# Block solve joins on four corners of the array with one joined tile per chunk, w0 loads and x_scr stores per pair of groups

## The chip, the cores and the metric

The kernel runs on one core of one Trainium2 chip. The metric is the device time of one execution in microseconds; for the kernel before the median of three runs is 1325.73 us (1323.58 to 1325.76).

## What is computed

A recurrent attention over 768 steps for 32 heads (4 batches of 8) with a state of 40x40 per head, and behind it two MLP layers of 320 to 2048 to 320 on all 3072 tokens, all in float32. The second layer uses an ELU in place of the squared ReLU.

```python
for t in range(S):
    y[:, :, t] = np.einsum('bhd,bhde->bhe', rt, state)
    Sa = np.einsum('bhde,bhe->bhd', state, at)
    state_decay = state * wt[:, :, None, :] - np.einsum('bhd,bhe->bhde', Sa, bt)
    state = state_decay + np.einsum('bhd,bhe->bhde', vt, kt)
x = attn_out.transpose(0, 2, 1, 3).reshape(B * S, H * D)
h = np.maximum(x @ w_in, 0.0); x = h * h @ w_out
h = x @ w_in2; g = np.where(h > 0, h, np.exp(np.minimum(h, 0)) - 1); out = g @ w_out2
```

## The kernel before

The 768 steps are cut into 12 chunks of 64 (`C`, `NC`), and the 32 heads into four groups `u` of 8 (`U`, `HU`); two groups form a pair `p`, and the members of a pair are told apart by `g = u % 2`. Within a chunk the recurrence becomes a triangular system per head, with a matrix of 64x64. A chunk goes through these stages:

- *prep*: running products of the decay (`scan`), scaled copies of a and r split into three bf16 planes and stored to DRAM, and k and b scaled (`kb_rows`).
- *gram*: for each group the 64x64 products (`gram`); the part for the solve is copied to `bs` and stored to `b_scr` by ACT's queue.
- *solve*: the system is cut into two halves of 32 and these into blocks of 16. `block_load` brings all 128 diagonal blocks (32 heads, four each) into a tile `w`, and fifteen `block_step`s on DVE invert them. `block_store` writes one inverse per half in transposed form to `n_scr` and both to `t_scr`, from where SP loads `n1` (tag nt) and the tiles `tb`, in which the inverse of each 32x32 half is put together. What is missing there is the block off the diagonal of each half: minus the product inverse, coupling, inverse. `block_join` makes it by two runs of small matmuls per chunk. The first run multiplies the coupling (`lz`, tag pb, 16 rows, 32 columns of which the left 16 are cleared by POOL) with `n1`; the second multiplies its result `x` with the inverse that stands in `tb`, and the result is copied into `tb`.
- *dynamic*: with the state at the chunk's start, `dyn_f`, `dyn_u`, `dyn_bu` and `dyn_u` again solve for a pair (by `tb`), `dyn_sp`, `dyn_ut` and `dyn_gh` make the second gram, `dyn_y` the outputs, `dyn_s` and `dyn_st` the new state. `w0` holds the decay products: `dyn_y` multiplies the output into it and stores it to `x_scr`, `dyn_s` reads its last column.
- *mlp1* and *mlp2*: the two layers, 24 passes over 256 tokens in float32r with hi and lo parts. They read `x_scr` and `x2_scr`.

In a run of the join `put` and `base` give the places. In the first run a head's two halves lie at rows and columns 0 and 32 of the array; in the second at 0 and 32 for groups with g = 0 and at 64 and 96 for those with g = 1. Each run has 64 matmuls for 32 heads, in two groups of 32 matmuls (`nc.group()`), and each group is copied out of PSUM by itself: two copies of 64 rows in the first run, four of 16 rows in the second. Both groups write one PSUM tile (`accA` for the first two chunks, then tag `at`).

The order of all instructions is written by a planner within the kernel. `at(...)` gives each step a due time from the tables `OFF`, `SHIFT` and `BIAS`; `flush` then simulates five engines and the DMA rings, takes at each engine the ready step with the smallest score, and fixes the resulting order for each engine. A `nc.group()` is one step that isn't broken up. `T_W2` and `T_CL` are the due times at which buffers of the attention's preparation are given to the second layer's weights. The buffer counts that matter here are `TB` (tiles `tb`, three of [128, 16, 32]) and `W0` (two of [40, 8, 65]). The matrix instructions of all stages stand in the trace under line 528, where the planner issues them.

Of the kernel before, what the change touches and what calls it, by code (L numbers as in the profile page):

```python
# [11 lines left out]
F32 = mybir.dt.float32  # L12
# [10 lines left out]
B, H, S, D = 4, 8, 768, 40  # L23
# [23 lines left out]
RP, TB, KB, KS = 1, 3, 3, 1  # L47
GS, LIMIT, FLOOR = 4, 2.0 ** 80, 2.0 ** -50
WPE = True
T_W2, T_CL = 176.1, 213.4  # L50
OFF = {
# [9 lines left out]
}  # L61
SHIFT = {
    "prep": [-252.4, -24.58, -12.17, -10.47, -1.272, -5.026, -6.748, -9.319, -3.061, -9.193, -7.383, -4.819],
# [1396 lines left out]
```

## Time and profile before

| | us |
|---|---|
| median of three runs | 1325.73 |
| profiled execution, its own time | 1321.71 |
| span of the profiled execution | 1319.9 |
| PE busy with matmuls | 1207.2 |
| ACT busy | 792.5 |
| DVE busy | 769.4 |
| POOL busy | 510.3 |

The span runs from the first to the last instruction; the profiled execution is one of its own and lies 4.0 us under the median. The granted clock of TensorE is 0.949 on average over the span. Times in the rows below count from the start of the span. An fp32 matmul of the program stands in the trace as two records, each with its weight load (PEld).

### The profile page before, as it was taken

Reading aid. Unit: us, or ns where it says so; the run is one execution under the profiler, and the core shown is the slowest. Engines: PE = TensorE matmul, PEld = TensorE weight load, DVE = VectorE, ACT = ScalarE, POOL = GpSimd, SP = SyncE. Lnnn points to the kernel's source line nnn. Section 1 sums busy time; section 2 is a strip of 40 time slices with the busy share of each in tenths; the row PEclk is TensorE's granted clock in tenths of the full one; section 3 lists DMA queues with packets and bytes.
Section 4 is the critical chain, followed back from the end, with each engine's and each line's share of the span. In section 5 each row is a group of like instructions: output and inputs, shape, how many; then the busy total and the mean of one; then the engine's idle time right before and its main releaser. Section 6 shows DMA issues by size and latency. Waiting matters only on the chain. (4 is left out here: it accounts for less than half of the span.)

```text
span 1319.9 us, 41548 instructions
## 1 busy us (share of the span) xinstructions
PE 1207.2 (91%) x17409; PEld 1105.7 (84%) x17409; DVE 769.4 (58%) x1434; ACT 792.5 (60%) x1536; POOL 510.3 (39%) x485
## 2 busy tenths in 40 slices
PE   2648779999998999999999999999999999999996
PEld 1536657889897898889888999999999999999995
DVE  6467866756575668665655645578744444444442
ACT  4556576565674657575655546455666666666663
POOL 2341241153363334364334224367633333333332
PEclk9996768897998799999999999999999999999998
DMA  8787786575777475765565434334200010000000
GB/s 268 189 222 207 179 253 153 126 187 150 185 195 164 104 203 130 196 138 160 129 160 136 103 77 135 123 103 124 65 21 20 22 30 21 21 21 22 16 11 18
DMA packets 239570, 157.99 MB, mean 120 GB/s; under 512 B 164112, under 2 KB 212624, under 8 KB 239376
## 3 DMA queue, kind: packets, MB, share of 16 engines
q1 hardware_dynamic: 213072, 148.18, 42.2%
q10 hardware_dynamic: 26304, 7.08, 2.8%
q8 instruction: 139, 2.28, 0.7%
q14 instruction: 55, 0.45, 0.1%
HBM read 114.52 MB, written 40.69 MB: 118 GB/s over the span
## 5 line engine op out<-in xcount | busy, mean ns | idle before, releaser
L528 PE MATMUL h<-xhi,w 128*128 128x256 f32 x1920 | 512.3, 298 | 2.9 <-DVE r L528 1.6
L528 POOL TENSOR_TENSOR glo<-r,ghi 128x512 fp32r<-128x512 f32 x192 | 254.0, 1324 | 413.9 <-ACT ghi L528 219.6
L528 PEld LDWEIGHTS h<-xhi,w 128*128 128x128 f32 x1920 | 357.8, 191 | 22.8 <-DVE r L528 12.7
L528 PE MATMUL h<-xlo,w 128*128 128x256 f32 x1152 | 324.4, 284 | 1.8 <-POOL xlo L528 1.6
L528 PEld LDWEIGHTS h<-xlo,w 128*128 128x128 f32 x1152 | 220.6, 191 | 2.7 <-POOL xlo L528 2.7
L528 ACT ACTIVATE r<-h 128x512 f32<-128x512 f32 x192 | 114.7, 597 | 139.6 <-PE h L528 117.4
L528 DVE SCALAR_TENSOR_TENSOR r<-e,r 128x512 f32<-128x512 f32 x96 | 81.3, 847 | 182.0 <-ACT r L528 180.9
L528 PE MATMUL accA<-w,ghi 128*128 128x320 f32 x768 | 179.1, 315 | 1.9 <-ACT ghi L528 1.9
L528 PE MATMUL accB<-w,ghi 128*128 128x320 f32 x768 | 178.2, 314 | 0.0
L528 DVE TENSOR_TENSOR r<-h,r 128x512 f32<-128x512 f32 x192 | 132.4, 689 | 74.9 <-ACT ghi L528 53.3
L528 PEld LDWEIGHTS accA<-w,ghi 128*128 128x128 f32 x768 | 124.9, 191 | 3.4 <-ACT ghi L528 2.8
L528 PEld LDWEIGHTS accB<-w,ghi 128*128 128x128 f32 x768 | 125.4, 191 | 0.4
L528 PE MATMUL accA<-w,glo 128*128 128x320 f32 x384 | 124.0, 323 | 1.0 <-POOLq L1392 0.6
L528 PE MATMUL accB<-w,glo 128*128 128x320 f32 x384 | 123.2, 321 | 0.0
L528 ACT CAST ghi<-r 128x512 fp32r<-128x512 f32 x96 | 59.0, 615 | 37.2 <-DVE r L528 20.5
L528 DVE SCALAR_TENSOR_TENSOR tt<-tt 128x1 f32<-128x1 f32 (+4 forms) x165 | 71.4, 433 | 15.9 <-DMA tt<-b_scr 8.5
L528 POOL TENSOR_TENSOR kd<-kbt,ks 128x320 f32<-128x320 f32 x42 | 38.1, 908 | 103.1 <-ACT ks L528 101.7
L528 PEld LDWEIGHTS accA<-w,glo 128*128 128x128 f32 x384 | 73.7, 192 | 2.8 <-POOL glo L528 1.1
L528 ACT ACTIVATE ghi<-r 128x512 fp32r<-128x512 f32 x96 | 60.6, 632 | 24.1 <-PE accB L528 21.0
L528 PEld LDWEIGHTS accB<-w,glo 128*128 128x128 f32 x384 | 73.4, 191 | 1.3
L528 ACT ACTIVATE r<-r 128x512 f32<-128x512 f32 x96 | 60.7, 632 | 2.0
L528 ACT COPY gx<-stk 120x1024 bf16<-120x1024 bf16 x48 | 48.5, 1011 | 22.1 <-PE stk L528 13.0
(157 smaller groups left out, 2159.7 us busy)
## 6 DMA issues: line engine op xcount, KB each, us to landing
gy<-ya_scr SPq DMA_DIRECT2D x144, 120.0 KB
rq<-r_scr SPq DMA_DIRECT2D x72, 240.0 KB
cs<-w SPq DMA_DIRECT2D x32, 512.0 KB
kbt<-kbt SPq DMA_DIRECT2D x12, 640.0 KB
cs<-w SPq DMA_DIRECT2D x16, 384.0 KB
b_scr<-bs ACTq DMA_DIRECT2D x48, 128.0 KB
ya_scr<-pl SPq DMA_DIRECT2D x12, 480.0 KB
r_scr<-pl SPq DMA_DIRECT2D x12, 480.0 KB
```

The source lines that it names most:

```text
L528: i = getattr(getattr(self.nc, name), op)(*a, **k)
```

## The change

The join is laid out anew. `b_scr` is filled in the order of `spot(u)`, so that the groups with g = 0 come first and those with g = 1 second, and `side(g)` names each half of the heads. `lz` and `n1` now take all 128 partitions: for each side and half the 16 rows lie at partitions 0, 32, 64 and 96. In both runs a step `n` issues four matmuls at the four corners (rows and columns 0, 32, 64, 96), for 16 values of `n`, in a single group of 64 matmuls. `lz` is packed without the cleared left half; its stationary is still 32 columns wide and reaches into the next head's columns, whose results aren't read. The second run reads the inverse from the right half of `n1` in place of `tb`, with 16 rows contracted in place of 32. For that `n_scr` has 32 columns, ACT's queue stores two kinds of inverse to it, and it is cleared once at the start; it has two buffers for the twelve chunks. The first run's result goes to a tile `xj` by one copy on ACT; the second's is copied out by two copies each on ACT and DVE. The two `tb` tiles of a chunk become one with two buffers (`TB`). `w0` is loaded for a pair of groups at once, with one buffer, and `x_scr` is stored for the pair after the second group's `dyn_y`. All numbers of the planner's tables are replaced.

```diff
--- before.py
+++ after.py
@@ -44,145 +44,146 @@
-RP, TB, KB, KS = 1, 3, 3, 1
+RP, TB, KB, KS = 1, 2, 3, 1
-T_W2, T_CL = 176.1, 213.4
+T_W2, T_CL = 177.1, 222.8
...
@@ -579,7 +580,7 @@
-    n_scr = [dram.tile([NH, 2, 16, 16], F32, name=f"n_scr{c}") for c in range(NC)]
+    n_scr = [dram.tile([NH, 2, 32, 32], F32, name=f"n_scr{c}") for c in range(2)]
@@ -813,6 +814,12 @@
+        def spot(u):
+            return u % 2 * 2 + u // 2
+
+        def side(g):
+            return slice(g * 2 * HU, (g + 1) * 2 * HU)
+
@@ -974,7 +981,7 @@
-            nc.scalar.dma_start(out=ap(b_scr[c][:], u * HU * HB, [[C, C], [HB, HU], [1, C]]), in_=bs[b])
+            nc.scalar.dma_start(out=ap(b_scr[c][:], spot(u) * HU * HB, [[C, C], [HB, HU], [1, C]]), in_=bs[b])
@@ -982,29 +989,29 @@
-            lz = get("pb", 0, [128, NH, 32])
-            n1 = get("nt", 1024, [64, NH, 16])
+            lz = get("pb", 0, [128, NH * HU + 16])
+            x = get("xj", 272, [128, 2 * HU, 16])
+            n1 = get("nt", 528, [128, 2 * HU, 32])
...
-            ex[c, "lz"], ex[c, "n1"], ex[c, "w"] = lz, n1, w
-            nc.gpsimd.memset(flat(lz)[0:64], 0.0)
+            ex[c, "lz"], ex[c, "xj"], ex[c, "n1"], ex[c, "w"] = lz, x, n1, w
+            nc.gpsimd.memset(lz[:, NH * HU:], 0.0)
...
-            for h in range(2):
-                tb = p1.tile([128, NH // 2, 32], F32, tag="tb", bufs=TB, name="tb")
-                ex[c, h, "tb"] = tb
+            ex[c, "tb"] = p1.tile([128, 2, 2 * HU, 32], F32, tag="tb", bufs=TB, name="tb")
...
-            for h in range(2):
-                o = 32 * h
-                nc.sync.dma_start(out=ex[c, "lz"][o:o + 16, :, 16:32], in_=ap(b_scr[c][:], o * C + o + 16, [[C, 16], [HB, NH], [1, 16]]))
-                for g in range(2):
+            for g in range(2):
+                k = g * 2 * HU * HB
+                for o in (0, 32):
...
-                        out=ex[c, h, "tb"][64 - 64 * g:96 - 64 * g, HU * g:HU * g + HU],
-                        in_=ap(b_scr[c][:], (2 * h + g) * HU * HB + 32, [[C, 32], [HB, HU], [1, 32]]))
+                        out=ex[c, "lz"][64 * g + o:64 * g + o + 16, :NH * HU].rearrange("p (n r) -> p n r", r=16),
+                        in_=ap(b_scr[c][:], k + o * C + o + 16, [[C, 16], [HB, 2 * HU], [1, 16]]))
+                nc.sync.dma_start(
+                    out=ex[c, "tb"][64 - 64 * g:96 - 64 * g, g], in_=ap(b_scr[c][:], k + 32, [[C, 32], [HB, 2 * HU], [1, 32]]))
@@ -1014,54 +1021,38 @@
-            w = ex[c, "w"]
+            w, n = ex[c, "w"], n_scr[c % 2]
...
-            nc.scalar.dma_start(out=n_scr[c].rearrange("n h t r -> (n h) t r"), in_=w[::2, 0])
+            for q, i in ((1, 1), (0, 0)):
+                nc.scalar.dma_start(out=ap(n[:], 16 * q, [[1024, 64], [32, 16], [1, 16]]), in_=w[q::2, i])
...
-            for h in range(2):
-                nc.sync.dma_start(out=ex[c, "n1"][32 * h:32 * h + 16], in_=n_scr[c][:, h].rearrange("n t r -> t n r"))
-            for u in range(U):
-                g = u % 2
-                nc.sync.dma_start(
-                    out=ex[c, u // 2, "tb"][64 * g:64 * g + 64, HU * g:HU * g + HU],
-                    in_=t_scr[c % 2][hs(u)].rearrange("n q r t -> (q r) n t"))
+            for g in range(2):
+                nc.sync.dma_start(out=ex[c, "n1"][64 * g:64 * g + 64], in_=n[side(g)].rearrange("n h t x -> (h t) n x"))
+            for g in range(2):
+                nc.sync.dma_start(out=ex[c, "tb"][64 * g:64 * g + 64, g], in_=t_scr[c % 2][side(g)].rearrange("n q r t -> (q r) n t"))
...
-            lz, n1 = ex[c, "lz"], ex[c, "n1"]
-            x = flat(lz)[:, :NH * 16].rearrange("p (n r) -> p n r", n=NH)
-
-            def run(rows, put, l, r, evict):
+            lz, x, n1, tb = ex[c, "lz"], ex[c, "xj"], ex[c, "n1"], ex[c, "tb"]
+
+            def run(rows, l, r):
...
-                    ps = ps_acc.tile([128, NH, 16], F32, tag="accA", name="join")
+                    ps = ps_acc.tile([128, 2 * HU, 16], F32, tag="accA", name="join")
...
-                    ps = ps_at.tile([128, NH, 16], F32, tag="at", name="join")
-                for k in range(2):
-                    with nc.group():
-                        for n in range(16 * k, 16 * k + 16):
-                            for o in (0, 32):
-                                nc.tensor.matmul(out=ps[put(o, n):put(o, n) + rows, n], lhsT=l(o, n), rhs=r(o, n), start=True, stop=True)
-                    evict(ps, k, slice(16 * k, 16 * k + 16))
-
-            def first(ps, k, n):
-                for g in range(2):
-                    o, m = 64 * g, slice(16 * k + HU * g, 16 * k + HU * g + HU)
-                    (nc.scalar.copy if k else nc.vector.tensor_copy)(out=x[o:o + 64, m], in_=ps[0:64, m])
-
-            def second(ps, k, n):
-                for g in range(2):
-                    o, m, h = 64 * g, slice(16 * k + HU * g, 16 * k + HU * g + HU), slice(HU * g, HU * g + HU)
-                    nc.scalar.copy(out=ex[c, k, "tb"][o:o + 16, h, 16:32], in_=ps[o:o + 16, m])
-                    nc.vector.tensor_copy(out=ex[c, k, "tb"][o + 32:o + 48, h, 16:32], in_=ps[o + 32:o + 48, m])
-
-            def base(o, n):
-                return o + 64 * (n // HU % 2)
-
-            def at_half(o, n):
-                return slice(base(o, n), base(o, n) + 32)
-
-            run(32, lambda o, n: o, lambda o, n: lz[o:o + 16, n], lambda o, n: n1[o:o + 16, n], first)
-            run(16, base, lambda o, n: x[at_half(o, n), n], lambda o, n: ex[c, n // 16, "tb"][at_half(o, n), n % 16, 16:32], second)
+                    ps = ps_at.tile([128, 2 * HU, 16], F32, tag="at", name="join")
+                with nc.group():
+                    for n in range(2 * HU):
+                        for o in range(0, 128, 32):
+                            nc.tensor.matmul(out=ps[o:o + rows, n], lhsT=l(slice(o, o + 16), n), rhs=r(slice(o, o + 16), n), start=True, stop=True)
+                return ps
+
+            ps = run(32, lambda p, n: lz[p, 16 * n:16 * n + 32], lambda p, n: n1[p, n, :16])
+            nc.scalar.copy(out=flat(x), in_=flat(ps))
+            ps = run(16, lambda p, n: x[p, n], lambda p, n: n1[p, n, 16:])
+            for g in range(2):
+                for o in (0, 32):
+                    k = slice(64 * g + o, 64 * g + o + 16)
+                    (nc.vector.tensor_copy if o else nc.scalar.copy)(out=tb[k, g, :, 16:], in_=ps[k])
@@ -1080,9 +1071,10 @@
-            w0 = p1.tile([D, HU, C + 1], F32, tag="w0", bufs=W0, name="w0")
-            ex[c, u, "w0"] = w0
-            nc.sync.dma_start(out=w0, in_=p_scr[c][:, hs(u)])
+            if u % 2 == 0:
+                ex[c, u // 2, "w0s"] = p1.tile([D, 2 * HU, C + 1], F32, tag="w0", bufs=W0 // 2, name="w0")
+                nc.sync.dma_start(out=ex[c, u // 2, "w0s"], in_=p_scr[c][:, pair(u)])
+            ex[c, u, "w0"] = ex[c, u // 2, "w0s"][:, hs(u % 2)]
@@ -1103,24 +1095,24 @@
-            f, tb, ps = ex[c, p, "f"], ex[c, p, "tb"], ex[c, p, "fa"]
+            f, tb, ps = ex[c, p, "f"], ex[c, "tb"], ex[c, p, "fa"]
...
-                        nc.tensor.matmul(out=ps[r, n], lhsT=tb[r, HU * g + n], rhs=f[r, n], start=True, stop=True)
+                        nc.tensor.matmul(out=ps[r, n], lhsT=tb[r, g, HU * p + n], rhs=f[r, n], start=True, stop=True)
...
-            f, tb, ps = ex[c, p, "f"], ex[c, p, "tb"], ex[c, p, "fa"]
+            f, tb, ps = ex[c, p, "f"], ex[c, "tb"], ex[c, p, "fa"]
...
-                            out=ps[64 * g + 32:64 * g + 64, n], lhsT=tb[k, HU * g + n], rhs=ex[c, 2 * p + g, "vu"][k, n], start=False, stop=(n == HU - 1),
+                            out=ps[64 * g + 32:64 * g + 64, n], lhsT=tb[k, g, HU * p + n], rhs=ex[c, 2 * p + g, "vu"][k, n], start=False, stop=(n == HU - 1),
@@ -1162,9 +1154,10 @@
-            nc.sync.dma_start(
-                out=x_scr[c][:, 2 * u:2 * u + 2].rearrange("e h (b t) -> e (h b) t", b=B),
-                in_=w0[:, :, :C])
+            if u % 2:
+                nc.sync.dma_start(
+                    out=x_scr[c][:, 2 * u - 2:2 * u + 2].rearrange("e h (b t) -> e (h b) t", b=B),
+                    in_=ex[c, u // 2, "w0s"][:, :, :C])
@@ -1230,10 +1223,12 @@
-            zero = p0.tile([128, NH, 32], F32, tag="pb", bufs=NBLK, name="zero")
-            nc.gpsimd.memset(flat(zero)[:, :512], 0.0)
+            zero = p0.tile([128, 512], F32, tag="nt", bufs=NBLK, name="zero")
+            nc.gpsimd.memset(zero, 0.0)
...
-                nc.sync.dma_start(out=t.rearrange("n q r t -> (n q) (r t)"), in_=flat(zero)[:, :512])
+                nc.sync.dma_start(out=t.rearrange("n q r t -> (n q) (r t)"), in_=zero)
+            for t in n_scr:
+                nc.scalar.dma_start(out=ap(t[:], 0, [[512, 128], [1, 512]]), in_=zero)
```

## Rows read from the trace of the kernel before

**Rows 1.** The page, parts 1 and 3: busy us (share); queue packets, MB.

```profile
span 1319.9 us, 41548 instructions
PE 1207.2 (91%) x17409; PEld 1105.7 (84%) x17409; DVE 769.4 (58%) x1434; ACT 792.5 (60%) x1536; POOL 510.3 (39%) x485
q8 instruction: 139, 2.28, 0.7%
```

**Rows 2.** Busy us by stretch: length, engines (x instructions), clock, DMA share, GB/s.

```profile
0.00:130.00 130.00, 70.59 (x956) 54.73 (x958) 78.93 (x157) 71.81 (x145) 41.74 (x49) 0.91 0.80 222
130.00:260.00 130.00, 109.78 (x2137) 89.66 (x2136) 94.47 (x207) 83.90 (x170) 35.23 (x34) 0.79 0.69 178
260.00:800.00 540.00, 522.46 (x10211) 475.09 (x10207) 333.12 (x703) 318.20 (x638) 216.89 (x211) 0.96 0.60 150
800.00:1320.00 520.00, 504.41 (x4120) 486.23 (x4117) 262.85 (x370) 318.60 (x586) 216.40 (x191) 0.99 0.17 48
```

**Rows 3.** Waits of PE: who, releaser, us in total, times, longest.

```profile
PE join L528 <- issue: 9.7, 6, 5.7
PE join L528 <- ACT pb L528: 1.3, 1, 1.3
```

**Rows 4.** Groups by line: operation, shapes, count, busy us, mean ns, idle before.

```profile
L528 PE MATMUL join<-nt,pb 16*32 16x16 f32 x1408 | 28.6, 183 | 3.9 <-DMA nt<-n_scr 3.1 <-DVE gh L528 0.8
L528 PE MATMUL join<-tb,pb 32*16 32x16 f32 x1408 | 20.2, 174 | 10.3 <-issue 8.5 <-ACT pb L528 1.3 <-DVE pb L528 0.4
```

**Rows 5.** Timeline, PE, 600 to 660 us: start, length, operation, shapes, records.

```profile
602.98 0.46 PE L528 MATMUL str<-ident,vs 40*40 40x40 f32 x8
613.17 1.19 PE L528 MATMUL join<-nt,pb 16*32 16x16 f32 x64
619.02 0.81 PE L528 MATMUL s<-vu,kbt 128*40 128x40 f32 x32
620.99 0.89 PE L528 MATMUL join<-tb,pb 32*16 32x16 f32 x64
```

**Rows 6.** Timeline, 288 to 300 us, PE around one group of the second run.

```profile
289.35 0.31 PE L528 MATMUL accA<-w,glo 128*128 128x320 f32 x1
289.58 0.89 PE L528 MATMUL join<-tb,pb 32*16 32x16 f32 x64
290.40 0.56 PE L528 MATMUL accB<-w,ghi 128*128 128x320 f32 x2
```

**Rows 7.** DMA issues: queue, count, KB each; the load for the first run.

```profile
nt<-n_scr SPq DMA_DIRECT2D x22, 32.0 KB
```

**Rows 8.** Instructions on tile w: SP's w0 loads, ns min/median/max.

```profile
L528 SPq DMA_DIRECT2D w<-p_scr x48: 273/318/2551, 21.3 to 839.6; - x48
```

**Rows 9.** Timeline, 405 to 432 us, PE's join; idle before in brackets.

```profile
418.50 2.25 PE L528 MATMUL join<-nt,pb 16*32 16x16 f32 x128
421.12 1.36 PE L528 MATMUL join<-tb,pb 32*16 32x16 f32 x104 [0.38 <-DVE pb L528]
428.15 0.51 PE L528 MATMUL join<-tb,pb 32*16 32x16 f32 x24 [5.67 <-issue]
```

**Rows 10.** DMA queues, 425.5 to 426.0 us: packets, MB, share of engines.

```profile
q8 instruction: 1, 0.02, 13.8%
```

**Rows 11.** Timelines of PE: where other join runs go on after an idle time.

```profile
107.73 0.69 PE L528 MATMUL join<-tb,pb 32*16 32x16 f32 x44 [0.67 <-issue]
158.84 0.34 PE L528 MATMUL join<-tb,free 32*16 32x16 f32 x11 [1.19 <-issue]
218.94 0.79 PE L528 MATMUL join<-tb,pb 32*16 32x16 f32 x55 [0.43 <-issue]
293.51 0.26 PE L528 MATMUL join<-tb,pb 32*16 32x16 f32 x7 [1.30 <-issue]
```

**Rows 12.** Busy time by stretch, columns as in rows 2, behind two stalls.

```profile
293.50:315.00 21.50, 21.49 (x284) 19.51 (x284) 8.16 (x28) 8.83 (x20) 6.92 (x6) 0.54 0.72 186
421.00:451.00 30.00, 23.20 (x363) 21.33 (x363) 17.37 (x44) 12.78 (x30) 11.62 (x12) 0.60 0.45 111
```

More of the change, by code (lines that the diff above doesn't have):

```diff
@@ L46 @@
 SUBV, SUBK, VC = 1, 0, 1
-RP, TB, KB, KS = 1, 3, 3, 1
+RP, TB, KB, KS = 1, 2, 3, 1
 GS, LIMIT, FLOOR = 4, 2.0 ** 80, 2.0 ** -50
 WPE = True
-T_W2, T_CL = 176.1, 213.4
+T_W2, T_CL = 177.1, 222.8
 OFF = {
[9 rows of a table removed]
[9 rows of a table added]
 }
 SHIFT = {
-    "prep": [-252.4, -24.58, -12.17, -10.47, -1.272, -5.026, -6.748, -9.319, -3.061, -9.193, -7.383, -4.819],
-    "gram": [-202, -7.468, -15.62, -13.63, -3.948, -6.708, -10.78, -9.453, -7.021, -13.38, -5.386, -8.988],
-    "solve": [-28.55, -6.792, -6.956, 2.77, 2.25, 3.314, 4.85, 8.249, 5.394, -1.603, -2.223, -3.919],
-    "dyn": [-7.115, -0.164, 3.141, 2.877, -0.4202, 0.4353, 1.525, 8.763, 6.207, 2.873, -0.4381, 2.331],
-    "mlp": [-10.63, -6.306, -5.107, -5.92, 1.545, -0.1849, -0.4791, -1.937, -0.9688, 15.42, 23.84, 67.31],
-    "w": [0.7824, 28.74, 9.338, -281.5, 595.9, 206.1, 37.91, 698.2, 70.89, 213.2, 242.8, -75.76],
-    "mlp2": [58.68, 193.7, 207.6, 396.4, 457.9, 483.3, 553.6, 587.1, 624.8, 641, 672.7, 697.4],
+    "prep": [-306.2, -104.1, -17.02, -11.91, -2.675, -7.126, -7.919, -9.366, -10.37, -10.99, -11.69, -10.21],
+    "gram": [-257.2, -10.75, -16.84, -17.01, -7.801, -9.024, -10.76, -15.37, -14.17, -16.76, -18.25, -0.3549],
+    "solve": [-40.11, 0.5233, -3.804, 3.07, 1.387, 4.686, 2.404, 1.274, 7.999, -0.3056, 2.541, 0.0884],
+    "dyn": [-5.829, 0.9955, 4.614, 3.102, 0.6603, 4.294, 1.335, 2.417, 6.503, 3.266, 1.248, 6.329],
+    "mlp": [-10.91, -7.632, -6.51, -0.05103, 4.447, 2.94, 1.894, 0.6392, 5.571, 33.09, 32.23, 63.08],
+    "w": [0.7774, 23.19, -173.8, -463, 811.6, 386.3, 335.8, 895.2, 77.26, 166.6, 300.2, -99.71],
+    "mlp2": [92.9, 289.3, 299.5, 535.5, 568.1, 610.4, 787.5, 829.7, 933.5, 966.3, 982.4, 1030],
@@ L70 @@
 }
 BIAS = {
-    "scan": [13.26, 6.176, -5.325, 0, -2.635, -5.793, 1.988, 28.93, 1.106, -1.397, -12.63, 8.316],
[107 rows of a table removed]
-    "out": [1.344, -2.018, 20.81, -1.778, 3.498, 62.02, 32.87, 20.64, 20.19, -2.632, 7.53, 18.95],
-    "rg": [-22.09, -29.07, -24.26, -86.91, -107.9, -26.03, -44.44, -5.98, -21.02, -164.5, -37.79, -30.08],
-}
-SWITCH, THIN, CHILL, BUSY = 0.09435, 7.919, 28.43, 0.6976
-YIELD = {"PE": (2.587e+06, 6.959, 80.92), "DVE": (0.1309, 2.937, 5.164e+09), "ACT": (0.2351, 0.03413, 686.2), "POOL": (0.0002282, 4.888, 2.397e+06), "SP": (136.9, 4.725, 220)}
@@ L185 @@
-HOLD = {"PE": (1.841, 924.1), "DVE": (0.7854, 9.898e+05), "ACT": (0.01352, 234.3), "POOL": (1.027e-05, 29.14), "SP": (0, 0.01961)}
+    "scan": [-14.45, -6.917, 6.823, -7.93, 1.19, -0.6704, 1.392, 28.81, -7.401, 2.702, 1.043, 0],
[108 rows of a table added]
+    "out": [-61.68, -3.645, 22.85, -7.648, 20.22, 20.36, -61.48, 10.61, -6.54, 8.011, 2.491, 8.861],
+    "rg": [-10.07, -35.66, -9.431, -49.51, -48.52, 2.42, -26.63, -56.25, 7.219, -76.09, 0.3756, -82.85],
+}
+SWITCH, THIN, CHILL, BUSY = 0.2357, 5.301, 46.48, 0.6436
@@ L186 @@
+YIELD = {"PE": (500, 6.153, 46.47), "DVE": (0.09153, 0.2352, 4.93e+07), "ACT": (0.2135, 0.0127, 1.728e+05), "POOL": (3.464e-05, 1.611e-05, 7.251e+07), "SP": (4.337, 0.1149, 313.7)}
+HOLD = {"PE": (1.462, 636.7), "DVE": (1.463, 7.172e+08), "ACT": (32.93, 22.84), "POOL": (2.07e-06, 1.21), "SP": (0, 5.371e-08)}
 CLOSE = 110.0
```

233 rows, old and new, of tables (BIAS, OFF) are left out of this document.

## The prediction

> **What bounds the kernel now.** I read the page first [rows 1]: PE is busy for 1207.2 us of a span of 1319.9 us, DVE and ACT for 58 and 60% of it. A share over the whole span mixes stages, so the second view is the busy time by stretch [rows 2]. In 0 to 130 us PE is idle for 59 us and in 130 to 260 us for 20 us, where the granted clock is 0.91 and 0.79: there the first two chunks wait for their own chains. From 260 to 800 us PE is idle for only 540 - 522.5 = 17.5 us at a clock of 0.96, and after 800 us it is dense, at 0.99, until the last drain. So from 260 us on the bound is PE's work: DVE, ACT and POOL stand at 62% or less there, and MLP matmuls are always queued as filler. A PE microsecond saved in a chunk is a microsecond off the end, and a transfer that is shortened is worth nothing by itself.
>
> Third, what PE waits for, of which the item that counts for this change is the join [rows 3]: 9.7 us in six waits, put down to "issue", which means that nothing the profile shows was awaited. The joins are also 28.6 + 20.2 us of PE time in the page's groups [rows 4], for the eleven chunks whose tiles have these names.
>
> **Part 1, the matmuls of the join.** The count stays: 64 matmuls in each of two runs per chunk, each seen as two records, so 128 records a run; only their places change, from two corners to four. In a warm stretch [rows 5] the 64 records of the first run (stationary 32 columns wide) take 1.19 us; without the last record's own 0.18 us that is 16.0 ns from one to the next. The second run (16 columns) takes 0.89 us, so 11.4 ns. Matmuls with 40 columns at two places stand (0.81 - 0.22) / 31 = 19 ns apart, and the transposes with 40 columns at one place (0.46 - 0.20) / 7 = 37 ns. Spacing thus goes with the width of the stationary and falls by half from one place to two. Whether it falls again from two to four no row shows. Upper bound of the gain: both runs at half, 128 x (8.0 + 5.7) ns = 1.75 us a warm chunk, 21 us for twelve. Lower bound: nothing. I take the first run down to the closest spacing that any row shows, 11.4 ns, and leave the second alone: 128 x 4.6 ns = 0.6 us a chunk, 7 us for twelve, 8 us with the first chunks that run at half the clock.
>
> The Trainium skill speaks against this part ("TensorE: Matmul & The Clock Gate", section "Wait — 56ns, not 53.3ns?"): matmuls never start less than about 25 ns apart, however small. The 11.4 ns row contradicts it for these records, and the measurement decides; by the page neither run could gain, and the sum would lose the 8 us.
>
> **Part 2, half as many groups.** Each run was two groups of 32 matmuls which the planner may place apart; it becomes one of 64. Entering costs 0.08 us: the 320-column matmul at 289.35 would let a successor start at about 289.50, and the join starts at 289.58. Leaving costs 0.09 us: the last record starts at 290.30, the next matmul at 290.40 instead of 290.31 [rows 6]. 24 groups fewer at 0.17 us: 4 us.
>
> **Part 3, evictions and clears.** Twelve copies a chunk become five, and POOL's clear of 64x1024 shrinks to 128x16. These engines have slack. PE itself waits little for such copies, once for 1.3 us [rows 3]. The single copy after the first run is a new serial step, but other groups fill PE meanwhile. I count -2 us.
>
> **Part 4, DMA.** Loads of w0 and stores of x_scr go from four to two a chunk, the tb loads from t_scr from four to two: six fewer issues on SP. The n_scr path grows: two stores instead of one on ACT's queue, and two loads of 128 KB instead of 32 KB [rows 7]. After 260 us DMA is at 0.60 or less and all of it hides behind MLP matmuls; if that cover were gone, 256 KB more at 150 GB/s would be 1.7 us a chunk. In the start little hides: the new zero fills of n_scr, two of 128x512 fp32, so 512 KB, take 2.4 us at 222 GB/s [rows 2], or nothing if they fall into a gap. The first join's extra 256 KB add 1.2 us; six issues at 0.32 us each [rows 8] give 1.9 us back. I count +2 us. With one w0 buffer a pair the next pair's load waits for the store after the second y. Queued behind it on SP would be the next chunk's loads, and the state update of the second pair waits for it; before, the load for the fourth group waited for the second group's store in just the same way, so only y of the third group starts later: 0, at most +4 us in the first two chunks.
>
> **Part 5, the stalls.** This is the term with the largest spread. At 421.12 us the second run breaks off after 104 records and goes on at 428.15: 5.67 us [rows 9]. It is no wait for data, since the break lies inside a group. An instruction packet (queue q8) moved at 425.5 us [rows 10]; the page counts 139 such packets for 2.28 MB [rows 1], so 16.4 KB each, one per 125 matmul records. PE ran out of instructions while other transfers filled the DMA engines. The same shows at 107.73, 158.84, 218.94 and 293.51 us [rows 11], and once more for the 0.4 us that are left of the 9.7. And the clock falls behind the large ones: from 293.5 to 315 us it is 0.54 and from 421 to 451 us 0.60 [rows 12], so for the most part the lower of its two levels, 1.2 in place of 2.4 GHz, which costs 21.5 x 0.46 + 30 x 0.40 = 22 us. Stalls and dips together take 7 + 22 = 29 of the 39 us that the stretch from 260 to 800 us loses. Four chunks had the first run in one piece of 128 records (100.82, 151.96, 209.30 and 418.50 us; the last is shown), and all four stalled in or before the second run, by 0.67, 1.19, 0.43 and 5.67 us; of the eight with split runs two did. The change makes every run one piece. Ends: no large stall, -29 us; 12 x 2.0 us (the mean of the four) instead of 9.7 us, +14 us, with one or two more dips of 11 us. I take 0, two dips as now: the replaced order decides where other transfers stand, and the row nearest to it is the present count.
>
> **Part 6, the planner's numbers** are all replaced, so the order moves everywhere. No row prices that. From 260 us on little but the joins is left to gain; in 0 to 260 us, with 79 us idle, it can go either way: 0, with ends of -10 and +10 us.
>
> **Sum.** -8 - 4 - 2 + 2 + 0 + 0 = -12 us. The profiled execution took 1321.7 us (span 1319.9), 4.0 us under the median of 1325.7; the forecast is 1321.7 - 12 + 4.0 = 1313.7, so 1314 us. 0.2%, about what a measurement of this kernel can tell from no change, is 2.7 us: faster means under 1323.1 and slower over 1328.4.
>
> **Rivals.**
> (a) *Instructions run short.* Every run is one piece of a whole packet's worth and the two runs come close together, so PE asks for two packets in some 4 us, at the pace of the run that stalled for 5.67 us. Stalls rise by 14 us and one further dip costs 11 us: 1314 + 25 = 1339. It decides once stalls and dips add more than the 12 us saved, which one more event like that of 421 us (5.7 + 12 us) does. For: four of four one-piece runs stalled. Against: three of these were 1.2 us or less.
> (b) *The stalls leave the warm stage.* Shorter runs and other neighbours: 1314 - 29 = 1285. For: six of the eight chunks with split runs show none at all. Against: these were split. The Trainium skill is on this side ("Runtime: NRT & Kernel Launch", section "Instruction fetch mechanics"): blocks of 16 KiB are fetched ahead and the fetch is hidden. The packet size agrees with 16.4 KB; that it is hidden, the 5.67 us contradict.
> (c) *The change doesn't do what it says.* The stationary loads go one after another, the first run stays at 16 ns: 1314 + 8 = 1322, at the edge of no change. For: the spacing follows the columns. Against: the step from 37 to 19 ns.
> (d) *Four corners really double both runs:* 1314 - 13 = 1301.
>
> **How the numbers follow.** Forecast 0.33 (own range 1306 to 1322), (a) 0.33, (b) 0.12, (c) 0.12, (d) 0.10. Faster: the forecast, (b), (d) and a third of (c), less 0.06 for a start that comes out worse: 0.53. Slower: (a) and 0.03 of that 0.06: 0.36. The rest, 0.11, is the same. The range leaves out the far half of (b) and the tail of (a): 1288 to 1345. Cases of both signs hold most of the chance; the forecast's own range stands above.
>
> **What would show it.** Join records 11.4 ns apart or less in the first run and 24 groups of 128 (steps 1 and 2); PE's "issue" wait at the join near 10 us and two stretches of low clock after 260 us (step 5); idle time in 0 to 260 us near 79 us (steps 4 and 6). The forecast is wrong if the "issue" wait is above 20 us or gone, or if the start moves by more than 10 us.

## The result, and the profile after

| | before | after |
|---|---|---|
| median, us | 1320.01 (20 runs) | 1331.87 (20 runs) |
| ratio | 1 | 1.0108 (95%: 1.0080 to 1.0136) |
| profiled execution, own time and span, us | 1321.71, 1319.9 | 1324.26, 1322.4 |
| join matmuls, eleven chunks, busy us | 48.8 | 30.0 |
| PE idle from 260 to 800 us | 17.5 | 31.2 |

The kernel is 12 us slower. The forecast was 1314 us, 12 us under the median of before that was then known; the time lies in the range (1288 to 1345), on the other side of the kernel before. The profiled execution of after is the fastest of its twenty, so its trace shows the smaller part of the 12 us. Its page, in the place of [rows 1] (busy us and share of the span):

```profile
span 1322.4 us, 41262 instructions
PE 1182.3 (89%) x17409; PEld 1085.9 (82%) x17409; DVE 765.5 (58%) x1386; ACT 782.6 (59%) x1500; POOL 499.6 (38%) x485
```

PE is busy for 24.9 us less than before, and its idle time is 27 us more. Where, the stretches of [rows 2] tell (length, then busy us of PE, PEld, DVE, ACT and POOL, granted clock, DMA share, GB/s):

```profile
0.00:130.00 130.00, 63.60 (x889) 49.44 (x890) 77.27 (x140) 69.64 (x141) 41.60 (x51) 0.73 0.82 226
130.00:260.00 130.00, 103.52 (x2191) 84.02 (x2190) 94.39 (x203) 81.60 (x163) 29.89 (x31) 0.79 0.75 186
260.00:800.00 540.00, 508.81 (x10213) 460.57 (x10212) 332.63 (x674) 314.97 (x611) 210.89 (x212) 0.97 0.64 154
800.00:1320.00 520.00, 506.41 (x4124) 491.88 (x4122) 261.25 (x371) 316.42 (x587) 217.19 (x192) 0.99 0.17 47
```

Before 260 us PE is idle for 92.9 us, against 79.6 us in [rows 2]; from 260 to 800 us for 31.2 us against 17.5 us. The two have nearly the same count of records in that stretch (10211 and 10213), and PE is busy for 13.7 us less: what the joins gave there came back as waiting.

The joins themselves gain more than was forecast. The groups by line (shapes, count, busy us, mean ns, idle before) and the timeline from 610 to 621 us, in the place of [rows 4] and [rows 5]:

```profile
L529 PE MATMUL join<-nt,pb 16*32 16x16 f32 x1408 | 15.3, 183 | 3.2 <-issue 1.6 <-DMA nt<-n_scr 1.6
L529 PE MATMUL join<-nt,xj 16*16 16x16 f32 x1408 | 14.7, 178 | 5.4 <-issue 3.3 <-ACT xj L529 2.0
```

```profile
610.52 1.23 PE L529 MATMUL join<-nt,pb 16*32 16x16 f32 x124 [0.43 <-DMA nt<-n_scr]
619.50 1.22 PE L529 MATMUL join<-nt,xj 16*16 16x16 f32 x128
```

The first run's records stand (1.23 - 0.18) / 123 = 8.5 ns apart, against 16.0 ns, the second's (1.22 - 0.18) / 127 = 8.2 ns, against 11.4 ns. And PE's waits, in the place of [rows 3] (total us, times, longest):

```profile
PE gram L529 <- issue: 5.1, 3, 3.0
PE join L529 <- issue: 5.0, 6, 1.6
```

The wait for instructions has not gone: over the whole span it is 14.0 us against 9.9 us, from 260 to 800 us 11.5 us against 7.4 us. In this execution it is shorter within the join, and what follows a join has it instead. The largest case (timeline of PE, 525 to 552 us):

```profile
531.27 1.35 PE L529 MATMUL join<-nt,pb 16*32 16x16 f32 x128
537.56 1.44 PE L529 MATMUL gram<-gy,gx 120*128 120x64 bf16 x24 [3.03 <-issue]
```

Between them stand 8 + 24 records of small bf16 matmuls and four of the MLP: 164 records in some 3 us, more than one packet of 125. PE then has nothing to run for 3.03 us, and the clock falls behind it (same columns as the stretches above):

```profile
537.00:548.00 11.00, 10.44 (x192) 9.86 (x192) 2.22 (x4) 4.42 (x8) 3.31 (x4) 0.53 0.47 125
```

### The profile page after: what moved, and what is told of

Same layout as the page of the kernel before. It is cut to its first block, busy times and chain, and to the rows that moved or that the text cites. A ratio compares the mean times of both kernels' runs of the same rounds, so it can differ in the third digit from the quotient of the medians.

```text
span 1322.4 us, 41262 instructions
## 1 busy us (share of the span) xinstructions
PE 1182.3 (89%) x17409; PEld 1085.9 (82%) x17409; DVE 765.5 (58%) x1386; ACT 782.6 (59%) x1500; POOL 499.6 (38%) x485
## 5 line engine op out<-in xcount | busy, mean ns | idle before, releaser
L529 POOL TENSOR_TENSOR glo<-r,ghi 128x512 fp32r<-128x512 f32 x192 | 257.2, 1341 | 465.2 <-ACT ghi L529 217.5
L529 DVE SCALAR_TENSOR_TENSOR r<-e,r 128x512 f32<-128x512 f32 x96 | 78.2, 814 | 177.2 <-ACT r L529 166.1
L529 DVE SCALAR_TENSOR_TENSOR tt<-tt 128x1 f32<-128x1 f32 (+4 forms) x165 | 79.2, 480 | 15.8 <-DMA tt<-b_scr 11.8
L529 PE MATMUL gram<-gy,gx 120*128 120x64 bf16 x1152 | 49.3, 205 | 25.5 <-DMA gy<-ya_scr 10.4
L529 POOL TENSOR_TENSOR kd<-kbt,ks 128x320 f32<-128x320 f32 x42 | 39.8, 946 | 79.6 <-ACT ks L529 77.3
L529 PEld LDWEIGHTS <-gx 120*128 120x128 bf16 x1152 | 43.8, 106 | 30.8 <-issue 12.9
```

Source lines behind the costliest of these rows:

```text
L529: i = getattr(getattr(self.nc, name), op)(*a, **k)
```

## Experiments

Three theories were open. **PE is the bound** (the prediction's ground): a PE us is a us at the end. **Instructions run short** (its rival a). **Order**: the replaced numbers of the planner put the instructions into another order, and that sets the time. Where an edit below is said to keep the order, it changes only what a step issues, and the traces show the same sequence of work on every engine.

### The two tables exchanged

`e1` is after's code with before's planner numbers, `e2` before's code with after's:

```diff
-T_W2, T_CL = 177.1, 222.8
+T_W2, T_CL = 176.1, 213.4
...
```

> The layout of the changed kernel (four corners, one joined tile, pairs for w0 and x_scr) with the planner's tables of the kernel before. Theory A, the loss of 12 us is one of the order that the new tables give (start 13 us more idle): this run is faster than the changed kernel and at or under the kernel before, 1305 to 1320 us. Theory B, the layout itself loses, because the denser joins run out of instructions: as slow as the changed kernel or slower, 1330 us or more, with more than 7 us of issue waits behind 260 us. Theory C, tables and layout are fitted to one another: slower than both kernels, 1335 us or more, whatever the layout is worth.

> The layout of the kernel before with the planner's tables of the changed kernel. Theory A: slower than the kernel before by at least the 12 us, so 1332 us or more, and by some 15 to 25 us slower than the changed kernel, whose joins take less PE time. Theory B: near the kernel before, 1315 to 1325 us. Theory C: slower than both, 1340 us or more.

Measured: 1343.92 us, ratio to before 1.0194 (1.0100 to 1.0287), and 1340.20 us, 1.0151 (1.0054 to 1.0249). The old layout loses some 20 us when it gets the other's numbers. The new one is slower than with its own numbers by some 11 us (1.0194 against 1.0108), which the interval of `e1` doesn't tell from nothing. So for the old layout at least, numbers and layout are fitted to one another, and part 6 of the prediction, which took the numbers at 0 with ends of 10 us, was too narrow.

### The join's pace at a fixed order

Four kernels keep the order and change the join alone. `e3` goes over the corners two at a time, `e5` one at a time, with the same 64 matmuls. In `f1` (on after) and `f2` (on before) wide matmuls take the place of 64 or 32 narrow ones; the first head's block serves for all heads of a matmul. `a0` is after itself, for a second trace.

```diff
 # e3
-                    for n in range(2 * HU):
-                        for o in range(0, 128, 32):
+                    for g in range(0, 128, 64):
+                        for n in range(2 * HU):
+                            for o in (g, g + 32):
 # e5, behind the group
+                k = nc.ops[-1].calls
+                nc.ops[-1].calls = k[0::4] + k[1::4] + k[2::4] + k[3::4]
 # f1, behind the group (f2: 256 or 128 columns for each group of 32)
+                nc.ops[-1].calls = [("tensor", "matmul", (), dict(
+                    out=flat(ps[o:o + rows]), lhsT=l(slice(o, o + 16), 0), rhs=r(slice(o, o + 16), slice(0, 2 * HU)),
+                    start=True, stop=True)) for o in range(0, 128, 32)]
```

> The changed kernel with its order of work on every engine, but within a run the matmuls of two corners (0 and 32) come first and those of the other two (64 and 96) second, so that only two corners alternate. Records should stand 16 and 11.4 ns apart again in place of 8.5 and 8.3, so twelve chunks need 16 us more of PE. If PE is the bound and saved PE time is saved time: 1348 us, 16 us above the changed kernel. If the saved time is given back to instruction fetch or to waits of the fixed order: within 4 us of it, with less issue wait and less low clock behind 260 us.

> The kernel after, once more beside the others, for a second profiled execution. If its losses are fixed by the order of its instructions, the same waits of PE for instructions (gram behind the join at 531 us with 3.0 us, fa behind the join at 487 us with 1.2 us) and the same stretches of low clock (near 428, 490, 537, 612 and 660 us) come back at the same places to within some us, and the time is 1332 +-5 us. If they are luck of one execution, they stand elsewhere or are gone.

> The kernel after with the same order on every engine, but each run of the join is four matmuls of 256 columns, one per corner, in place of 64 matmuls of 16: every head's coupling is multiplied by the first head's block, so the results are not those of the reference. 240 records fewer per chunk and run pair, 2 x 120 matmul records, so about two instruction packets of 125 records fewer per chunk. PE work of a run: 0.45 us if the four corners go at once (1.3 us a chunk and 15 us in all less than after), about 1.7 us if one after another (14 us more). Theory 'instructions run short': the issue waits of PE from 260 to 800 us (11.5 us in after) fall under 4 us and two or more of the low stretches behind them go, so the time falls 20 us or more further than by the PE work alone: about 1295 to 1300 us in the first case. Theory 'order': only the PE work counts, and it counts by half as with two corners: about 1324 us in the first case, 1340 us in the second, with waits at other names.

> The same in the kernel before, its order unchanged: each group of 32 matmuls of the first run is two matmuls of 256 columns, each group of the second run four of 128 columns; the results are not those of the reference. Some 240 records fewer per chunk. PE work of the join falls from about 4.1 us a chunk to some 1.6 us if two corners go at once: 30 us in all. Theory 'PE is the bound': 30 us off the end, 1290 us, and 20 us more if the stall at 421 us and its low clock go with the instructions. Theory 'order': the instructions that follow wait for other engines instead, and half or less of it arrives: 1305 us or more.

> The kernel after with the same order on every engine, but the 64 matmuls of a run are sorted by corner, 16 at each in turn, so that successive ones stand at one place. If the spacing goes with the number of places, the records stand about 23 to 32 ns apart in place of 8.5 and 8.3 ns: a chunk's join takes 6 to 8 us in place of 2.4 us, 50 to 60 us more PE work in all. Theory 'a PE us is a us at the end': the time rises by as much as the PE work, to 1385 us or more. Theory 'the chain and the order set part of it': it rises by half to three quarters, 1357 to 1375 us, and PE's idle time between 260 and 800 us shrinks below the 31 us of after.

Measured, beside the two kernels (join busy in eleven chunks; idle and instruction waits of PE from 260 to 800 us):

| kernel | join us | idle us | wait for instructions us | time us | ratio to before (95%) |
|---|---|---|---|---|---|
| e5, one corner | 84.1 | 6.4 | 0.4 | 1373.28 | 1.0403 (1.0354 to 1.0452) |
| e3, two corners | 43.4 | 24.0 | 8.3 | 1342.63 | 1.0169 (1.0064 to 1.0274) |
| a0, four corners | 30.2 | 30.4 | 11.8 | 1337.42 | 1.0116 (1.0072 to 1.0161) |
| f1, wide | 15.4 | 38.5 | 0.0 | 1319.96 | 0.9979 (0.9946 to 1.0013) |
| before | 48.8 | 17.5 | 7.4 | 1323.10 | 1 |
| f2, before wide | 24.3 | 28.7 | 0.3 | 1308.22 | 0.9880 (0.9850 to 0.9910) |

`e3` was timed in another series, in which before stood at 1320.85 us; its ratio is what compares. The rows behind the ends of the table: groups by line, of `e5`, `f1` and `f2` in turn,

```profile
L529 PE MATMUL join<-nt,pb 16*32 16x16 f32 x1408 | 48.9, 185 | 0.0
L529 PE MATMUL join<-nt,xj 16*16 16x16 f32 x1408 | 35.2, 175 | 0.4 <-issue 0.4
```

```profile
L529 PE MATMUL join<-nt,pb 16*32 16x256 f32 x88 | 8.1, 397 | 1.5 <-DMA nt<-n_scr 1.5
L529 PE MATMUL join<-nt,xj 16*16 16x256 f32 x88 | 7.3, 401 | 2.9 <-ACT xj L529 2.9
```

```profile
L528 PE MATMUL join<-nt,pb 16*32 16x256 f32 x88 | 14.7, 407 | 3.5 <-DMA nt<-n_scr 2.2 <-DVE gh L528 0.8 <-DVE pb L528 0.5
L528 PE MATMUL join<-tb,pb 32*16 32x128 f32 x176 | 9.6, 285 | 5.2 <-DMA gy<-ya_scr 3.0 <-ACT tb L528 1.5 <-DVE pb L528 0.5
```

and their stretches from 260 to 800 us in the same order:

```profile
260.00:800.00 540.00, 533.57 (x9736) 489.35 (x9731) 329.82 (x673) 311.96 (x605) 205.76 (x207) 0.93 0.63 151
```

```profile
260.00:800.00 540.00, 501.50 (x8083) 446.14 (x8082) 330.30 (x672) 314.72 (x612) 208.37 (x211) 0.97 0.64 155
```

```profile
260.00:800.00 540.00, 511.32 (x8321) 451.37 (x8321) 334.48 (x709) 324.50 (x652) 217.16 (x215) 0.97 0.62 154
```

Three things follow.

*A PE us is not a us at the end.* From `e5` to `a0` the joins take 53.9 us less and the time falls by 35.9 us, two thirds; from `e3` to `a0` 13.2 us less, and the ratios differ by 0.0053, so 7 us, half (the intervals allow nothing or all of it). In both steps a part is lost to the waits for instructions, which rise to 11.8 us. Between `e5` and `f1` these stay at 0.4 us or less, and there 68.7 us less give 53.3 us, eight tenths (by the intervals of the ratios 0.7 to 0.9). From before, which has 7.4 us of them, to `f2` 24.5 us less give 14.9 us, six tenths (0.5 to 0.8). The column leaves out the twelfth chunk, whose tile has another name; with it the two shares are 0.71 and 0.56. The table shows where the rest stays: with each step down in the joins PE's idle time from 260 to 800 us goes up, 6.4, 24.0, 30.4, 38.5 us, though every kernel of the first four has the same order. Over the whole span, in which all four do the same MLP work, it is 104.5, 126.3, 140.8 and 149.2 us (span less busy time of PE). In `f1` none of it is a wait for instructions; PE waits for DVE, ACT and transfers. From 260 to 800 us PE is thus the bound for only part of the time, though it is busy for 93 to 99% of it in these kernels.

*The shortage of instructions goes with the pace.* At the same order and count of records it is 0.4 us at one corner, 8.3 at two and 11.8 at four, and 0 when the records go. That these are waits for instruction packets the traces show directly. In `f1` PE has 2880 records fewer and queue q8 moves 116 packets in place of 139, so 125 records each: the packets are PE's. For the wait of 3.03 us in after, which ends at 537.56 us, the packet starts at 535.11 us and lands at 536.07 us (DMA queues, 535 to 536 us):

```profile
q8 instruction: 1, 0.02, 6.0%
```

In the traces of all nineteen kernels of this case PE has 132 waits of over 0.6 us that are put down to "issue"; 129 of them end 1.1 to 1.7 us after such a packet has landed, and of its 820 other waits of that length 52 do. The packets come no closer than 3.07 us from start to start in any of these traces, so 125 records each 3.07 us, 25 ns a record, is the fastest supply seen. One packet lasts 125 x 8.4 ns = 1.05 us at four corners, and 3.0 to 3.7 us at one corner, at 24 to 29 ns.

`f1` gains 17.5 us on `a0` for 14.8 us of join time. At six to eight tenths of a PE us these give 9 to 12 us, so the other 6 to 9 us are put down to the shortage, an estimate: the 17.5 us alone are uncertain by some 7 us. In before, `f2` gets 14.9 us for 24.5 us of PE, no more than six to eight tenths of it (15 to 20 us), so no cost of the shortage shows there.

*Something else separates the two kernels.* Without the shortage (0.0 and 0.3 us), and with 8.9 us less of join time, after (`f1`) is still 11.7 us behind before (`f2`). With six to eight tenths of the 8.9 us, what separates them is 17 to 19 us, uncertain by some 6 us by the intervals.

`a0` had 11.8 us of instruction waits in the stretch where after had 11.5; the largest now stands within a join (3.5 us), the longest at `gram` is 0.9 us. The sum comes back with the order; each place doesn't.

### w0 per group again

```diff
-            if u % 2 == 0:
-                ex[c, u // 2, "w0s"] = p1.tile([D, 2 * HU, C + 1], F32, tag="w0", bufs=W0 // 2, name="w0")
+            w0 = p1.tile([D, HU, C + 1], F32, tag="w0", bufs=W0, name="w0")
```

and the loads and stores likewise, on after.

> The changed kernel with w0 loaded and x_scr stored per group of 8 heads again, two buffers (the planner orders anew around it). If the single pair buffer delays the recurrence: 5 to 15 us faster than the changed kernel, with less idle time of PE in 0 to 260 us. If it is hidden, as forecast: within 4 us, apart from what another order is worth, which the runs so far put at up to 10 us either way.

Measured: 1373.12 us, 1.0418 (1.0322 to 1.0515). The stretch from 260 to 800 us:

```profile
260.00:800.00 540.00, 494.74 (x9701) 447.97 (x9702) 315.89 (x653) 307.47 (x596) 201.21 (x205) 0.92 0.63 150
```

Half a thousand records fewer than after get done in this stretch, with 17.5 us of instruction waits and a clock of 0.92. The edit moves every step's place, so this doesn't price the pairing; it shows how far another order can lie.

### The start

After has done less of the second stage by 260 us. The records of the first MLP matmul (`h`) in that time, for before, `f2`, after and `f1` in turn (busy stretch of this tile alone):

```profile
0.00:260.00 260.00, 15.35 (x80) 11.99 (x80) 2.77 (x4) 2.99 (x5) 0.85 0.75 200
```

```profile
0.00:260.00 260.00, 16.38 (x80) 12.91 (x80) 2.77 (x4) 3.00 (x5) 0.77 0.76 201
```

```profile
0.00:260.00 260.00, 12.54 (x64) 9.15 (x64) 1.38 (x2) 1.18 (x2) 0.76 0.79 206
```

```profile
0.00:260.00 260.00, 12.37 (x64) 8.96 (x64) 1.38 (x2) 1.81 (x3) 0.80 0.80 208
```

80 against 64. The accumulations of the MLP lag more: 20 records each of accA and accB in before against 6 in after. Here is accA on PE alone, before and after; then, from 800 us on, `h` and accA that are left to do, before and after in turn; then their spacing (timeline of after):

```profile
0.00:260.00 260.00, 5.89 (x20) 0.85 0.75 200
0.00:260.00 260.00, 1.63 (x6) 0.76 0.79 206
```

```profile
800.00:1320.00 520.00, 346.73 (x2000) 0.99 0.17 48
800.00:1320.00 520.00, 348.63 (x2027) 0.99 0.17 47
800.00:1320.00 520.00, 192.96 (x762) 0.99 0.17 48
800.00:1320.00 520.00, 196.04 (x768) 0.99 0.17 47
```

```profile
608.40 0.28 PE L529 MATMUL h<-xhi,w 128*128 128x256 f32 x1
608.52 0.31 PE L529 MATMUL accA<-w,glo 128*128 128x320 f32 x1
608.67 0.46 PE L529 MATMUL accB<-w,ghi 128*128 128x320 f32 x2
```

At 0.12 us for a record of `h` and 0.15 us for one of accA or accB, after is 16 x 0.12 + 28 x 0.15 = 6 us behind at 260 us and 27 x 0.12 + 12 x 0.15 = 5 us at 800 us (accB has accA's counts); its span is 2.5 us longer. These are estimates from the rows. So in these two traces the lag stands at 260 us already, and from there on after keeps pace and no more: its longer idle time uses up its shorter joins.

Two waits offered themselves. The first scan starts at 9.25 us, waiting for wx, where before's starts at 6.89 us: the fills of `n_scr` go ahead of it. And in the second chunk `fa` waits for `tb`, whose copies stand on ACT behind conversions that wait for weights (timelines of after, ACT and PE):

```profile
174.09 0.65 ACT L529 ACTIVATE cs<-cs 128x512 f32<-128x512 f32 x1 [1.59 <-DMA cs<-w]
174.65 0.34 ACT L529 COPY tb<-join 16x256 f32<-16x256 f32 x1
...
175.05 0.33 PE L529 MATMUL fa<-f,tb 32*32 32x40 f32 x2 [3.86 <-ACT tb L529]
177.55 1.27 PE L529 MATMUL fa<-f,tb 32*32 32x40 f32 x30 [2.17 <-ACT tb L529]
```

`x1b` takes the fills away, `x2` puts the copies of the first three chunks ahead on ACT and DVE, `x3b` does both; all else keeps its order.

```diff
 # x1b
-            for t in n_scr:
-                nc.scalar.dma_start(out=ap(t[:], 0, [[512, 128], [1, 512]]), in_=zero)
+                nc.ops[-1].calls = [("sync", "dma_start", (), dict(
+                    out=ex[c, "n1"][64 * g + 32 * h:64 * g + 32 * h + 16],
+                    in_=n[side(g)][:, h, :16].rearrange("n t x -> t n x"))) for h in range(2)]
 # x2, in the planner, for the copies into tb of c < 3
+        for o, p in self.ahead:
+            o.start = min(o.start, p.start + 0.001)
```

> The kernel after with the same order, without the two zero fills of n_scr at the start (512 KB); the inverse is loaded by two transfers of its 16 used rows per side and half in place of one of 32 rows, half the bytes and one more issue. In after the first scan starts at 9.25 us, waiting for wx, in before at 6.89 us. Theory 'the fill delays the first load': the scan is back at 6.9 to 7.3 us, and the first grams 2.2 us earlier. If that lasts to the end, the time falls by 2 to 3 us (1329 to 1330); by 'the first 260 us are made up for later', by nothing.

> The kernel after with PE, POOL and SP in the same order; for the first three chunks the four copies of the joined blocks into tb stand on ACT and DVE ahead of the conversions of the second layer's weights that they stood behind. In after the second run of the second chunk ends at 169.3 us and fa waits until 175.05 and 177.55 us for the ACT copies of tb, which stand behind conversions that wait for cs<-w. Theory 'start chain': the wait of fa for ACT tb before 260 us falls from 7 us to under 2 us, the state update of that chunk (s at 189.3 us, 174.6 in before) comes 6 us or more earlier, and the time falls 5 to 10 us, to 1322 to 1327 us. By 'made up for later' the update comes earlier and the time stays at 1332 +-5 us.

> Both edits together. Theory 'the start sets the loss': the ledger of the first 260 us is back at the kernel before's, and the time falls by 8 to 12 us, to 1320 to 1324 us, level with before. By 'made up for later' 1329 to 1332 us.

Measured: 1332.07 us, 1.0092 (1.0046 to 1.0137); 1337.53 us, 1.0150 (1.0102 to 1.0198); 1333.96 us, 1.0095 (1.0060 to 1.0130). Both edits do what they say. The scan in `x1b` (timeline of DVE), and the wait of `fa` in `x2`, 7.3 us in after:

```profile
7.05 1.51 DVE L529 TENSOR_TENSOR_SCAN rs<-wx,starts 128x650 f32<-128x650 f32 x1 [7.05 <-DMA wx<-wx]
```

```profile
PE fa L531 <- ACT tb L531: 1.0, 2, 0.6
```

But the state update of the second chunk, at 189.3 us in after and 174.6 us in before, comes at 188.3, 188.0 and 185.0 us, and `x3b` has done no more by 260 us than after (`h` alone again):

```profile
0.00:260.00 260.00, 12.44 (x61) 9.07 (x61) 1.38 (x2) 1.20 (x2) 0.80 0.77 202
```

So the theory that these two waits are the start's loss falls: another wait takes their place, as in `x2`, where `fa` waits 4.2 us for vu in place of 0.9 us in after. That a better start would reach the end is neither shown nor excluded, since the start did not become better.

### Nudged orders

Every number of `BIAS` is moved by a random amount, the same one in both layouts: two draws of 0.25 of the planner's unit (about 1 us), one of 0.05.

```diff
+for NAME, SEED in zip(sorted(BIAS), np.random.RandomState(1).randn(len(BIAS), NC)):
+    BIAS[NAME] = [x + 0.25 * y for x, y in zip(BIAS[NAME], SEED)]
```

> The kernel before, each of the 1332 numbers of BIAS moved by a random amount (normal, 0.25 of the planner's unit, 1 us; first draw), so that its order is no longer the one that its numbers were fitted to. Theory 'order': a nudged order costs as much as replaced tables did (12 to 23 us), so 1330 to 1345 us, and the two nudged layouts lie within 6 us of one another or the new one ahead. Theory 'layout': nudges cost the same few us in both, and after's layout stays 12 us behind before's.

> The kernel after with the first draw's nudges, the same ones as in the kernel before. By 'order' 1330 to 1345 us, level with the nudged kernel before or below it by the 8 to 10 us that the four corners give at the end; by 'layout' some 12 us above it.

> The same with a second draw: by 'order' 1330 to 1345 us, and the difference between the two draws tells how far one order lies from the next, some 5 to 10 us.

> The kernel after with the second draw. As with the first: by 'order' level with the nudged kernel before or up to 10 us below, by 'layout' some 12 us above it.

> The kernel before with a third draw of nudges, five times smaller (0.05 of the planner's unit, 0.2 us). If the time follows the size of the nudge, it is within 3 us of before, 1320 to 1326 us. If any change of the order costs what another draw would, it is 6 to 30 us above it like the first two draws.

> The kernel after with the same small nudges. If the layout is what costs, it stays 10 us or more above the nudged kernel before, near 1335 us, as in the first two draws (38 and 9 us); if the numbers are, the two come within 6 us of one another or the order turns round.

| draw | before, time and ratio (95%) | after, time and ratio (95%) | wait for instructions, 260 to 800 us |
|---|---|---|---|
| 1 | 1352.74, 1.0227 (1.0163 to 1.0290) | 1390.76, 1.0507 (1.0442 to 1.0572) | 7.5 and 23.6 |
| 2 | 1329.53, 1.0046 (0.9971 to 1.0121) | 1338.63, 1.0131 (1.0067 to 1.0196) | 5.9 and 14.6 |
| 3, small | 1326.40, 1.0048 (0.9999 to 1.0096) | 1365.76, 1.0308 (1.0225 to 1.0391) | 4.8 and 12.1 |

The stretch from 260 to 800 us of the third draw, before's layout and after's:

```profile
260.00:800.00 540.00, 514.13 (x10176) 466.15 (x10176) 335.18 (x700) 316.94 (x631) 220.81 (x213) 0.97 0.60 150
```

```profile
260.00:800.00 540.00, 505.18 (x9707) 455.24 (x9706) 314.69 (x657) 308.25 (x601) 197.36 (x204) 0.92 0.64 152
```

In each draw the new layout is the slower one, by 38, 9 and 39 us, although its joins are the shorter ones; the 9 us of the second draw lie within the noise of four runs each. The size of the nudge says little: 0.2 us moves after by some 30 us and before by 4 to 6 us. So "order" alone, by which the two should have come level, does not hold; in two of three draws the new layout bears a change of its order worse. In all orders with its own kind of numbers its instruction waits are higher, 11.5 to 23.6 us against 4.8 to 7.5 us; with the new numbers the old layout has 11.5 us too (`e2`), so the order counts beside the pace. Where the time is long the clock of this stretch is low (0.89 in after's first draw).

## Why the prediction was wrong

**Part 1** was right in its mechanism and too small: 8.5 and 8.2 ns in place of the 11.4 ns it took for both, so 18.8 us of PE in eleven chunks where it counted 8 us in twelve. At the same order two corners take 43.4 us and four 30.2 us, so the corners are the cause. Rival (d)'s doubling came nearly true in the first run (16.0 to 8.5 ns) and not in the second (11.4 to 8.2 ns); rival (c) falls. The rule of the Trainium skill that the prediction set against this part ("TensorE: Matmul & The Clock Gate", section "Wait — 56ns, not 53.3ns?", starts about 25 ns apart at the least) is contradicted more widely still, by 8.2 ns.

**Parts 2 and 3** (fewer groups, fewer copies) were not measured by themselves.

**Part 4**: the fill of `n_scr` was put at 2.4 us; the first scan came 9.25 - 6.89 = 2.36 us later. It did not reach the end: without it the time stayed at 1332 us. The pairing of w0 stays unpriced.

**The step that failed most** is part 6, which put the replaced numbers at 0, with ends of 10 us, because no row priced them. The runs show 17 to 19 us in its place, for order and the rest of the layout together: that is what after lies behind before when no instructions run short and each us of join time is counted at its worth (`f1` against `f2`). The numbers alone cost the old layout some 20 us (`e2`). Part 6 named the start, and there PE's idle time rose by 13.3 us, more than the prediction allowed. The clock of the first 130 us (0.73 in place of 0.91) is not a mark of the layout: the same after had 0.84 there in `a0`, and `f2`, in before's layout, 0.72. That "from 260 us on little but the joins is left to gain" overlooked that there is something to lose.

**Part 5** took no change in stalls. The waits for instructions rose by 4 us, inside its ends, and rival (a) named the mechanism: by `f1` the shortage costs after 6 to 9 us, an estimate, and in before no cost shows, where (a) gave 25. What (a) missed is that the place is not fixed at the joins: after had 5.0 of its 14.0 us there, `a0` 9.0 of 14.2 us, and the rest stood at other matmuls. The longest single wait shrank from 5.7 to 3.0 us (3.5 us in `a0`). The Trainium skill's hidden fetch ("Runtime: NRT & Kernel Launch", section "Instruction fetch mechanics") is not borne out by these waits, 14.0 us in after and 14.2 us in `a0`.

**The ground of the prediction** fails too: "A PE microsecond saved in a chunk is a microsecond off the end." The stretch from 260 to 800 us is busy for 97% in before, but the share doesn't say that the rest of the chain can come earlier; six to eight tenths of a saved us arrive. The joins' 18.8 us were therefore worth 11 to 15 us, an estimate. That is more than the 8 us forecast for them, so this step by itself did not turn the sign.

**The sum as measured.** The joins give -11 to -15 us, the shortage takes some 6 to 9 us back; that alone would make after 2 to 9 us faster. The remaining 14 to 21 us belong to the order and the rest of the layout, and `f1` against `f2` says the same. The lag of 6 us at 260 us is a visible part. Which piece of it (paired w0 and x_scr, the larger transfers, the longer copies into `tb`, or numbers that sit at a narrow spot) stays open: each of these edits moves the order too, and one order lies 4 to 53 us from the next. Part of the 12 us comes with a lower granted clock: over all executions that have a clock on record its mean is 0.944 in before (64) and 0.934 in after and `a0` (26), and within the executions of either kernel 0.01 less goes with 4 to 7 us more. Whether the clock lengthens the time there or the waiting lowers the clock, no run separates. Of the kernels that compute the whole, none is faster than before.

## What to carry to other kernels

Before a saving on a busy engine is counted in full, lengthen that work at a fixed order and see how much arrives: at a busy share of 97% six to eight tenths did. Many tiny matmuls at a fast pace need their instructions supplied at that pace; count records per us against the packets (here 125 records each 3.07 us at the closest), not only the time they take. Where a planner's numbers are fitted to a layout, compare layouts over several nudged orders, since a single order can lie tens of us from its neighbour.

## What was not expected of the hardware

Records of fp32 matmuls with 16 rows contracted and 16 moving columns stand 8.2 to 8.5 ns apart when successive matmuls go to four corners; each matmul of the program is two records, so 16 to 17 ns a matmul. At one corner a record takes (2.86 - 0.19) / 91 = 29 ns with a stationary of 32 columns and (2.37 - 0.18) / 92 = 24 ns with 16 (timeline of PE in `e5`, granted clock 0.99 and 0.87 there):

```profile
559.85 2.86 PE L529 MATMUL join<-nt,pb 16*32 16x16 f32 x92
567.76 2.37 PE L529 MATMUL join<-nt,xj 16*16 16x16 f32 x93
```

And a run of 128 records that takes 1.35 us, with 36 more behind it, was followed by 3.03 us without instructions, and the 11 us from 537 us on ran at a clock of 0.53.
